# Softmax steps cut into parts between adding steps, and eight columns' sums moved from TensorE to VectorE and the crossbar

## The chip, the cores and the metric

The kernel runs on one core of one Trainium2 chip. The metric is the device time of one execution in microseconds (us); the median of several executions is quoted. The engines are TensorE (PE; its weight loads are listed as PEld), VectorE (DVE), ScalarE (ACT), GpSimd (POOL) and SyncE (SP), besides the DMA engines. The "crossbar" is the DMA path that transposes a tile while it moves it. "PE's use of unit u" means the start of PE's first matmul that reads unit u's transposed tile.

## The reference, cut to what matters

```python
# x: 8 x 4160 x 192, weight_gen: 8 x 4160 x 8 x 7
w = exp(weight_gen - max) ; w = w / (sum over the 7 taps + 1e-9)
y[b, s, h, :] = sum over k of w[b, s, h, k] * x_padded[b, s + k, h, :]     # causal window of 7
h1, h2 = y @ moe_w1, y @ moe_w2                                           # 192 -> 1024
out = maximum(h1, h2) @ moe_w_out                                         # 1024 -> 192
```

## The kernel before

The 33280 rows lie as 128 partitions by 260 columns, in batches of 16 columns (batch 16 has 4). A unit is a piece of a batch: 4 columns in batches 0 and 1 (units 0 to 7), 8 columns later (units 8 to 35), 4 in the last (unit 36). For each batch ScalarE takes exp of the seven taps' logits, DVE sums them (`red`), ScalarE takes Ln of the sums, DVE subtracts it from the logits (`shift`), and ScalarE's second exp (`weights`) gives the normalised weights `en_t` in bf16. For each unit DVE multiplies the seven shifted windows of x by the weights (`mul`) and sums the seven products in three adds (`adds`), and the crossbar turns `y_t` into `yt`:

```python
    def adds(b, o, first=False):
        ...
        nc.vector.tensor_tensor(out=taps(0, 1, 3), in0=taps(0, 1, 3), in1=taps(3, 1, 3), op=ALU.add)
        if first:
            return
        ...
        nc.vector.tensor_tensor(out=taps(0, 2, 2), in0=taps(0, 2, 2), in1=taps(1, 5, 2), op=ALU.add)
        nc.vector.tensor_tensor(out=_sub(y_ts[b], ...), in0=taps(0, 1, 1), in1=taps(2, 1, 1), op=ALU.add)
```

For the first 32 columns the crossbar is not used: DVE does only the first add (`first=True`) or none, and `sum_transpose` on PE sums the four remaining taps (all seven where DVE added none) and transposes them in one go, by matmuls with an identity; ScalarE copies the result to `yt`.

PE then computes h2 - h1 and ScalarE its ReLU, in groups of three tiles (a tile is one column's worth of work), and PE adds y @ (w1 @ w_out) and relu(h2 - h1) @ w_out, which together are the output. ScalarE copies the results out of PSUM and issues the stores. ScalarE carries out its queue in order: ReLUs, result copies, the softmax's exp and Ln all stand in one line.

What runs ahead is written into the loop over tiles by `extra(t)`:

```python
        if s == 0 and b + 1 < NB:
            c = b + 1
            mul(c, 0)
            if c + 1 < NB:
                shift(c + 1)
            adds(c, 0)
        if s == 8 and b + 2 < NB:
            mul(b + 1, 8)
            if b + 3 < NB:
                red(b + 3)
            adds(b + 1, 8)
        ...                                   # weights(c, 0), weights(c, 8) at tiles 8 and 12 of a batch
        if s == 14 and 3 < b + 3 < NB:
            ln(b + 3)
```

The softmax here doesn't subtract the row's maximum and nothing guards it: scores larger than these inputs give would overflow.

## Time and profile before

| | before |
|---|---|
| time, median (range) | 418.81 us (418.5 to 419.28, 4 runs) |
| busy: PE / DVE / ACT | 403.7 / 378.0 / 359.8 us of a span of 417.0 |
| DVE's last `y_t` ends | 385.1 us |
| DVE for 16 columns | 23.84 us |
| slack between landing of `yt` and PE's use, units 8 / 22 / 30 | 10.7 / 6.0 / 0.13 us |

The first line below is from the page's chain of work that ended last, by engine (share of the span). The others are from the table of waits: who waited for what, total us, number of waits, the longest.

```profile
DVE 73%; PE 17%; issue 4%; ACT 3%; DMA 2%; SPq 1%; DVEq 0%
```

```profile
ACT rd_t L260 <- PE hd L250: 30.3, 70, 0.8
...
PE op_ps L302 <- ACT o_t L346: 2.5, 6, 0.5
...
PE hd L250 <- ACT rd_t L260: 0.9, 3, 0.3
```

ScalarE waits for PE, in small pieces; PE hardly waits at all. Yet the chain that led to the last instruction runs through DVE for 73% of the span. Both are true: DVE has no pause for 360 us and PE has next to none, and at unit 30 they meet: `yt` lands 0.13 us before PE's use of it, and PE waits 0.24 us.

### The profile page before, as it was taken

Reading aid. Unit: us, or ns where it says so; the run is one execution under the profiler, and the core shown is the slowest. Engines: PE = TensorE matmul, PEld = TensorE weight load, DVE = VectorE, ACT = ScalarE, POOL = GpSimd, SP = SyncE. Lnnn points to the kernel's source line nnn. Section 1 sums busy time; section 2 is a strip of 40 time slices with the busy share of each in tenths; the row PEclk is TensorE's granted clock in tenths of the full one; section 3 lists DMA queues with packets and bytes.
Section 4 is the critical chain, followed back from the end, with each engine's and each line's share of the span. In section 5 each row is a group of like instructions: output and inputs, shape, how many; then the busy total and the mean of one; then the engine's idle time right before and its main releaser. Section 6 shows DMA issues by size and latency. Waiting matters only on the chain.

```text
span 417.0 us, 15881 instructions
## 1 busy us (share of the span) xinstructions
PE 403.7 (97%) x7369; PEld 326.8 (78%) x7369; DVE 378.0 (91%) x177; ACT 359.8 (86%) x416; POOL 69.0 (17%) x102
## 2 busy tenths in 40 slices
PE   7989999999999999999999999999999999999995
PEld 7878899777777778777787777877778677777795
DVE  5999999999999999999999999999999999999000
ACT  5898989999999899898989899899998898887871
POOL 1510101221201122212112232200113221120000
PEclk9999999999999999999999999999999999999999
DMA  8965427867569756875866669557674787685213
GB/s 235 260 168 169 108 68 169 183 153 129 144 151 181 192 151 163 207 147 153 201 149 147 168 127 242 142 163 198 142 209 64 165 202 151 128 163 115 97 49 144
DMA packets 60242, 65.68 MB, mean 157 GB/s; under 512 B 47601, under 2 KB 48497, under 8 KB 60176
## 3 DMA queue, kind: packets, MB, share of 16 engines
q0 software_dynamic: 8128, 24.11, 28.3%
q1 hardware_dynamic: 46720, 15.30, 21.5%
q10 hardware_dynamic: 5328, 25.27, 15.8%
q8 instruction: 57, 0.93, 0.9%
q14 instruction: 9, 0.07, 0.1%
HBM read 35.96 MB, written 25.56 MB: 148 GB/s over the span
## 4 chain that ended last, share of the span: by engine, by line
DVE 73%; PE 17%; issue 4%; ACT 3%; DMA 2%; SPq 1%; DVEq 0%
DVE m_t L157 36%; DVE m_t L172 15%; DVE m_t L177 11%; PE op_ps L290 8%; PE hd L250 5%; DVE sum_t L132 3%; DVE y_t L179 3%; DVE wg_t L140 3%; DMA ws1T<-in_moe_w_dram 2%; PE op_ps L302 2%; ACT rd_t L260 1%; PE hdp L250 1%; PE yps L218 1%; ACT en_t L148 0%; SPq L480 0%
## 5 line engine op out<-in xcount | busy, mean ns | idle before, releaser
L260 ACT ACTIVATE rd_t<-hd 128x1024 bf16<-128x1024 f32 (+1 forms) x206 | 234.6, 1183 | 30.8 <-PE hd L250 30.3
L290 PE MATMUL op_ps<-wo,rd_t 64*128 64x192 bf16 x4160 | 210.3, 243 | 0.1
L290 PEld LDWEIGHTS <-rd_t 64*128 64x128 bf16 x4160 | 180.1, 94 | 16.2 <-ACTq L323 0.3
L250 PE MATMUL hd<-yt,wd 64*128 64x512 bf16 (+1 forms) x1584 | 187.2, 360 | 1.1 <-ACT rd_t L260 0.9
L157 DVE TENSOR_TENSOR m_t<-xb_t,en_t 128x10752 bf16<-128x10752 bf16 (+1 forms) x37 | 187.5, 5070 | 0.2 <-ACT en_t L148 0.2
L250 PEld LDWEIGHTS <-wd 64*128 64x128 bf16 x1776 | 92.8, 94 | 42.3 <-issue 1.4
L194 POOL CAST gate<-yt 128x1 f32<-128x1 bf16 x29 | 33.2, 1146 | 280.8 <-DMA yt<-y_t 280.8
L172 DVE TENSOR_TENSOR m_t<-m_t 128x4608 bf16<-128x4608 bf16 (+1 forms) x34 | 79.5, 2339 | 0.1
L346 ACT COPY o_t<-op_ps 128x384 f32<-128x384 f32 (+1 forms) x99 | 56.9, 585 | 8.2 <-PE op_ps L290 8.1
L302 PE MATMUL op_ps<-w,yt 64*128 64x192 bf16 x780 | 55.3, 243 | 3.2 <-ACT o_t L346 2.5
L302 PEld LDWEIGHTS <-yt 64*128 64x128 bf16 x780 | 38.6, 94 | 20.1 <-issue 5.6
L177 DVE TENSOR_TENSOR m_t<-m_t 128x3072 bf16<-128x3072 bf16 (+1 forms) x29 | 50.2, 1730 | 1.0
L148 ACT ACTIVATE en_t<-wg_t 128x896 bf16<-128x896 f32 (+1 forms) x37 | 34.1, 935 | 1.9 <-ACT o_t L346 1.2
L179 DVE TENSOR_TENSOR y_t<-m_t 128x1536 bf16<-128x1536 bf16 (+1 forms) x29 | 27.4, 944 | 1.0
L336 DVE COPY o_t<-op_ps 128x192 f32<-128x192 f32 x1 | 0.4, 358 | 27.9 <-ACT o_t L336 27.9
L115 POOL DMA_DIRECT2D xb_t<-in_x_dram x32 | 17.2, 539 | 24.8 <-DVE m_t L157 16.1
L132 DVE TENSOR_REDUCE sum_t<-e_t 128x128 f32<-128x896 f32 (+1 forms) x17 | 17.6, 1037 | 2.9 <-ACT e_t L127 2.9
L127 ACT ACTIVATE e_t<-wg_t 128x896 f32<-128x896 f32 (+1 forms) x17 | 15.8, 928 | 3.3 <-DMA wg_t<-in_weight_gen_dram 2.8
L140 DVE TENSOR_TENSOR wg_t<-wg_t,sum_t 128x896 f32<-128x896 f32 (+1 forms) x17 | 17.7, 1043 | 0.8 <-ACT sum_t L135 0.8
L260 ACT ACTIVATE rd_t<-hdp 128x1024 bf16<-128x1024 f32 x16 | 15.7, 1027 | 1.5 <-PE hdp L250 0.5
L218 PE MATMUL yps<-ident,m_t 128*64 128x128 bf16 x492 | 15.3, 220 | 0.3 <-DVE m_t L157 0.2
L218 PEld LDWEIGHTS <-m_t 128*64 128x64 bf16 x492 | 14.1, 110 | 1.9 <-issue 1.1
(45 smaller groups left out, 85.6 us busy)
## 6 DMA issues: line engine op xcount, KB each, us to landing
out_dram<-o_t ACTq DMA_DIRECT2D x28, 768.0 KB, 4.3
xb_t<-in_x_dram POOLq DMA_DIRECT2D x28, 384.0 KB, 4.9
wg_t<-in_weight_gen_dram POOLq DMA_DIRECT2D x14, 448.0 KB, 6.3
xb_t<-xb_t POOLq DMA_DIRECT2D x16, 288.0 KB, 5.4
out_dram<-o_t ACTq DMA_DIRECT2D x8, 384.0 KB, 3.2
wg_t<-in_weight_gen_dram SPq DMA_DIRECT2D x2, 448.0 KB, 5.3
xs<-in_x_dram SPq DMA_DIRECT2D x2, 384.0 KB, 6.8
xb_t<-in_x_dram POOLq DMA_DIRECT2D x1, 768.0 KB, 6.8
```

The lines of the kernel that those rows point to most:

```text
L148: nc.scalar.activation(out=_sub(en_ts[b], o * WGC * 2, [[2 * N, K], [2, N], [1, 2]]), in_=_sub(wg_ts[b], o * WGC, [[1, K], [K, N], [0, 2]] ...
L157: nc.vector.tensor_tensor(out=m_t[:, K * o * D:K * (o + n) * D], in0=_sub(xb_ts[b], o * D, [[D, K], [1, n * D]]), in1=_sub(en_ts[b], o * W ...
L172: nc.vector.tensor_tensor(out=taps(0, 1, 3), in0=taps(0, 1, 3), in1=taps(3, 1, 3), op=ALU.add)
L177: nc.vector.tensor_tensor(out=taps(0, 2, 2), in0=taps(0, 2, 2), in1=taps(1, 5, 2), op=ALU.add)
L179: nc.vector.tensor_tensor(out=_sub(y_ts[b], o * D, [[64, 2], [P, 3 * w // 2], [1, 64]]), in0=taps(0, 1, 1), in1=taps(2, 1, 1), op=ALU.add,)
L194: nc.gpsimd.tensor_copy(out=gate, in_=yt[:, 0:1])
L218: nc.tensor.matmul(yps[half(j), k * P:(k + 1) * P], lhsT=m_t[:, at:at + 64], rhs=ident, start=(t == taps[0]), stop=(t == taps[-1]), skip_g ...
L250: nc.tensor.matmul(hid_out(t, f, j), lhsT=wd[half(j), s * F + f * P:s * F + (f + 1) * P], rhs=_sub(yt_ts[u][half(j), :], (s + j) % 3 * P, ...
L260: nc.scalar.activation(out=rd[:, k * 1024:(k + n) * 1024], in_=hd[:, at:at + n * 1024], func=AF.Relu)
L290: return nc.tensor.matmul(op_out(c), lhsT=rd[half(r), k * 1024 + at:k * 1024 + at + P], rhs=wo[half(r), f * D:(f + 1) * D], start=False, s ...
L302: nc.tensor.matmul(op_out(c + j), lhsT=yt_ts[u][half(j), (3 * i + (s + j) % 3) * P:(3 * i + (s + j) % 3 + 1) * P], rhs=w10[half(j), s * D: ...
L346: nc.scalar.copy(out=_sub(o, c % 24 * D, [[D, len(qs)], [h * D, 2], [1, D]]), in_=_sub(tile_, at + (qs[0] - p) * D, [[D, len(qs)], [512, 2 ...
```

## The change

The intent: (a) a softmax step set between two adds that depend on one another hides the second one's wait for the first, so the shift is cut into three parts and the reduction into two, one ahead of each add. (b) With the time won, DVE sums columns 24 to 31 (units 6 and 7) wholly and the crossbar moves them, which frees PE of two `sum_transpose` calls and ScalarE of two copies. (c) Ln is issued two tiles later from batch 6 on, because the reduction ends later now.

```diff
+    def part(b, i, of):
+        n = BATCHES[b][1]
+        h0, h1 = n * i // of * H, n * (i + 1) // of * H
+        return slice(h0, h1), h0 * K, [[K, h1 - h0], [1, K]]
 ...                                     # red(b, i, of) and shift(b, i, of) work on such a part
-    def adds(b, o, first=False):
+    def adds(b, o, first=False, beside=lambda i, of: None):
 ...                                     # beside(0, 3), beside(1, 3), beside(2, 3) ahead of the adds
     def rest_of_1():
-        adds(1, 8, True)
+        adds(1, 8)
     def end_of_1():
-        adds(1, 12, True)
+        adds(1, 12)
-        6: (lambda: (weights(2, 8), ln(3), sum_transpose(6, LEFT)), lambda: load_x(3, 0, 8)),
-        7: (lambda: sum_transpose(7, LEFT), none),
+        6: (lambda: (weights(2, 8), ln(3), transpose(6)), lambda: (transpose(7), load_x(3, 0, 8))),
 ...
+        at = 14 if t <= 16 * 3 else 16
+        c = (t - at) // 16 + 3
+        if (t - at) % 16 == 0 and 3 < c < NB:
+            ln(c)
-            if c + 1 < NB:
-                shift(c + 1)
-            adds(c, 0)
+            adds(c, 0, beside=lambda i, of: shift(c + 1, i, of) if c + 1 < NB else None)
-            if b + 3 < NB:
-                red(b + 3)
-            adds(b + 1, 8)
+            adds(b + 1, 8, beside=lambda i, of: red(b + 3, i, 2) if b + 3 < NB and i < 2 else None)
-        if s == 14 and 3 < b + 3 < NB:
-            ln(b + 3)
```

## The prediction

> **What bounds the kernel now.** I read the page's busy shares first, then the table of waits, then the timelines of VectorE (DVE), ScalarE (ACT) and TensorE (PE).
>
> ```profile
> PE 403.7 (97%) x7369; PEld 326.8 (78%) x7369; DVE 378.0 (91%) x177; ACT 359.8 (86%) x416; POOL 69.0 (17%) x102
> ```
>
> Three engines are nearly full, so the question is who waits for whom. The table of waits has almost nothing for PE and DVE, but two small rows tell that they are coupled:
>
> ```profile
> PE hd L250 <- DMA yt<-y_t: 0.2, 1, 0.2
> ...
> ACT sum_t L135 <- DVE sum_t L132: 3.9, 4, 1.4
> ```
>
> DVE makes each unit of eight columns (`y_t`), the crossbar moves it into `yt`, PE uses it. Following each unit through the trace, I took the landing of `yt` and PE's first matmul with it. The slack between them is 10.7 us for unit 8 (lands 65.1, used 75.8), 7.7 us for unit 14, 6.0 us for unit 22, 1.8 us for unit 28, 0.5 us for unit 29 and 0.13 us for unit 30 (lands 329.44, used 329.58); units 31 to 35 have 0.7 to 3.3 us and the last one 10.8 us. PE thus starts with a lead of DVE's results that it uses up, because DVE needs 23.84 us for 16 columns (its multiplications start at 47.66, 71.49, 95.33 us) and PE about 22.9 us at full speed. DVE has no pause above 0.04 us from 25 to 385 us. PE is the bound by a hair, and DVE stands right behind it by unit 30.
>
> One pair of units on DVE, late in the run (start, duration in us):
>
> ```profile
> 339.40 1.08 DVE L140 TENSOR_TENSOR wg_t<-wg_t,sum_t 128x896 f32<-128x896 f32 x1
> 340.40 2.55 DVE L172 TENSOR_TENSOR m_t<-m_t 128x4608 bf16<-128x4608 bf16 x1
> 342.99 1.76 DVE L177 TENSOR_TENSOR m_t<-m_t 128x3072 bf16<-128x3072 bf16 x1
> 344.78 0.96 DVE L179 TENSOR_TENSOR y_t<-m_t 128x1536 bf16<-128x1536 bf16 x1
> 345.65 5.75 DVE L157 TENSOR_TENSOR m_t<-xb_t,en_t 128x10752 bf16<-128x10752 bf16 x1
> 351.32 0.38 DVE L132 TENSOR_REDUCE sum_t<-e_t 128x32 f32<-128x224 f32 x1
> 351.62 2.54 DVE L172 TENSOR_TENSOR m_t<-m_t 128x4608 bf16<-128x4608 bf16 x1
> ```
>
> Start-to-start times count here, not durations. An instruction that needs nothing of the one before it starts 0.08 us before that one ends (the add at 340.40 in front of an end at 340.48); a dependent one starts 0.04 us after the end (342.99 after 342.95). A dependence thus costs 0.12 us.
>
> **What the Trainium skill says.** "Perfetto Trace Analysis", section on the DVE / Act engine instruction: the profiled time runs to the write's acknowledgement, while the next instruction may already begin when the ALUs are done. This trace agrees: that is the 0.08 us overlap, and a dependent successor loses it. "Vector Engine (DVE) Microarchitecture Reference", section 5.2: about 75 ns per instruction after queue overlap, plus 1.04 ns per column. The trace agrees: start to start, 224 elements take 0.30 us and 896 take 1.00 us, so 1.04 ns each and a fixed 0.07 us. "VectorE: DVE Perf Modes", the section on the DRAIN, says a semaphore after each instruction costs nothing extra; the 0.12 us here disagrees, and the measurement decides. "Perfetto Trace Analysis", the section on optimizing Scalar/DVE operations, recommends breaking up instructions where the engine is not saturated; this DVE is.
>
> **The change part by part.**
>
> (1) Parts on DVE. The shift of 896 elements becomes 280, 280 and 336, one ahead of each add: 0.07 x 3 + 0.93 = 1.146 us for 1.00, so +0.146. It breaks two dependences (first to second add, second to third), each worth 0.12: -0.24. Net -0.096. The reduction becomes two halves: +0.073, one dependence broken, -0.12; net -0.05. A batch of 16 columns gains 0.146 us, and some 13 batches give -1.9 us of DVE by the end.
>
> (2) Columns 24 to 31 (units 6 and 7) wholly on DVE. The first add of 2304 elements took 1.27 us start to start (46.39 to 47.66). With dependent followers, as in the last unit, it is 1.39, then 0.99, then 0.48: 2.86 us. Twice +1.59 gives +3.18 us on DVE, between 41 and 51 us, where it delays everything later on DVE. I call DVE's delay D: 3.18 us at batch 3's shift, less 0.146 a batch, so 1.6 at batch 14, 1.4 at batch 15 and 1.3 at the end.
>
> (3) The same on PE and ACT: these sums and transposes vanish,
>
> ```profile
> 46.92 1.53 PE L218 MATMUL yps<-ident,m_t 128*64 128x128 bf16 x48
> ...
> 51.58 1.53 PE L218 MATMUL yps<-ident,m_t 128*64 128x128 bf16 x48
> ```
>
> 1.46 us start to start each, 2.9 us of PE, and two ACT copies of 0.8 us. So from 53 us PE and ACT run 2.9 us earlier than before. With PE at 97% one is tempted to book 2.9 us. But this is a lead over DVE, and the lead is what runs out later.
>
> (4) Results of the softmax come later within a unit. For batches of 16, `en_t` of columns 0 to 7 reads the first two shift parts (560 of 896 elements; its 448 lie within them, and in the built program only the second half waits for DVE anew). The second part ends 0.36 + 2.47 + 0.44 = 3.27 us after the first starts, against 1.08: +2.2 us. The reduction's end moves from 1.08 to 0.54 + 2.47 + 0.62 = 3.62: +2.5 us. Ln is put off by two tiles, from batch 6 on, to allow for this, but in groups of three tiles that moves it by a whole group for some batches and not at all for batches 8, 11 and 14.
>
> ACT runs its queue in order, so a late shift or reduction stalls the ReLUs behind it, and PE after them. Slack before the change, measured in the trace:
>
> ```profile
> 339.68 1.88 ACT L260 ACTIVATE rd_t<-hd 128x2048 bf16<-128x2048 f32 x1
> 341.58 1.04 ACT L148 ACTIVATE en_t<-wg_t 128x896 bf16<-128x896 f32 x1
> 342.52 1.01 ACT L260 ACTIVATE rd_t<-hd 128x1024 bf16<-128x1024 f32 x1
> 343.46 0.80 ACT L346 COPY o_t<-op_ps 128x768 f32<-128x768 f32 x1
> ```
>
> This `en_t` (batch 15) starts 1.10 us after its shift ended at 340.48. After the change the two parts end at 340.48 + 1.43 + 2.2 = 344.1, so it cannot start before: ACT is then 2.5 us later than before, whatever lead it had. Ln of batch 14 (306.54, reduction ended 304.72) comes out alike: 304.72 + 1.62 + 2.54 = 308.9, 2.3 us later. `en_t` of batch 12 (slack 2.97) gives 1.1 us later, the landing of unit 30 gives D = 1.5 less 0.13, so 1.4 us later. These are limits on the same clock; they don't add. The latest wins: 2.5 us.
>
> Sum: ACT can absorb little. The copy at 343.46 ends at 344.26 and PE takes the bank at 344.54, so 0.2 us. After that PE has no idle time to catch up with except 0.3 us at 353.3, where ACT waited for the last batch's reduction; Ln of that batch now comes a group later. The end moves by 2.5 - 0.2 - 0.3 = +2.0 us: 418.8 + 2.0 = 420.8 us.
>
> **The rivals.**
>
> PE decides, and its 2.9 us are gained: 415.9 us. For it: 97% busy, and waits for `yt` of 0.2 us in the whole run. Against it: those 0.2 us at unit 30 show that PE can't run earlier there than DVE lets it; with D positive there is nothing to take.
>
> The broken dependences are worth more than 0.12 us, so that D is gone before unit 28 or so: then 417 to 418.5 us. For it: parts as fine as these have no example in this trace but the 224-element ones. Against: the fixed 0.07 us fits both kinds of instruction.
>
> Only the landing of `yt` counts, since ACT's stall hides in its 14% idle time: +1.4 us, less the 0.3, so about 419.9 us. For it: ACT waits 30 us for PE in 70 small pieces. Against: in the group of 341 us ACT has 0.2 us to give.
>
> The crossbar's landing grows, from two more transposes and a second load of batch 3's first half, which the new transpose of unit 6 issues in addition to the old one: landing varies between 2.7 and 7.4 us already. Those additions lie at 45 to 60 us, where slack is 10 us; no effect, unless phases shift late: up to 423 us.
>
> **Range and chances.** The central path gives 420.8, the DVE-only path 419.9, so I say 420.6. A stall that hides wholly and a larger gain per part would make 418; two stalls that do not overlap with one another, or later landings, 422.6. No path reaches 2% (8.4 us): faster 0.01, same 0.97, slower 0.02.
>
> **What would show it.** DVE's last `y_t` should end near 386.4 (385.07 before); a pair of units should take 23.7 us instead of 23.84. PE should be 2.9 us early for unit 8 and lose this lead by some 260 us; ACT should show new waits for DVE's `wg_t` (batches 12 and 15) and `sum_t` (8, 11, 14) of 1 to 2 us each, and PE waits for ACT behind them. I am wrong if PE keeps its lead to the end, if parts cost clearly other than 0.07 us more each, or if `en_t` waits for nothing.

## The result, and the profile after

The changed kernel took 421.25 us (420.84 to 421.84, 4 runs) against 418.81. The ratio is 1.0058, with a 95% interval of 1.0041 to 1.0076: by the threshold of 2% the same, by the interval slower by about 2.4 us. Ratios here are the mean time of one kernel's fast runs over that of the other's fast runs of the same rounds, so not quite the ratio of the medians.

The page after, busy shares and chain by engine:

```profile
PE 401.5 (96%) x7273; PEld 324.6 (77%) x7273; DVE 380.1 (90%) x222; ACT 358.6 (85%) x414; POOL 70.2 (17%) x106
...
DVE 68%; PE 20%; issue 4%; DMA 4%; ACT 2%; SPq 1%; DVEq 0%
```

PE has 2.2 us less to do, DVE 2.1 us more, and the span is 3.0 us longer (420.06 against 417.03). The work that was saved lay on an engine that did not get to use it.

The table of waits after:

```profile
ACT sum_t L142 <- DVE sum_t L139: 6.4, 6, 1.4
...
PE op_ps L313 <- ACT o_t L357: 4.2, 9, 0.6
...
ACT en_t L155 <- DVE wg_t L147: 1.3, 2, 0.6
...
PE hd L261 <- DMA yt<-y_t: 1.2, 1, 1.2
```

Against before: ScalarE's waits for DVE's sums rose from 3.9 to 6.4 us, waits for DVE's shift are new, PE's waits for ScalarE's copies rose from 2.5 to 4.2 us, and its wait for `yt` from 0.2 to 1.2 us.

DVE in the timeline of the changed kernel, the same unit as in the prediction's excerpt (start, duration in us):

```profile
340.46 0.44 DVE L147 TENSOR_TENSOR wg_t<-wg_t,sum_t 128x280 f32<-128x280 f32 x1
340.82 2.55 DVE L181 TENSOR_TENSOR m_t<-m_t 128x4608 bf16<-128x4608 bf16 x1
343.29 0.44 DVE L147 TENSOR_TENSOR wg_t<-wg_t,sum_t 128x280 f32<-128x280 f32 x1
343.65 1.75 DVE L187 TENSOR_TENSOR m_t<-m_t 128x3072 bf16<-128x3072 bf16 x1
345.32 0.50 DVE L147 TENSOR_TENSOR wg_t<-wg_t,sum_t 128x336 f32<-128x336 f32 x1
345.74 0.95 DVE L190 TENSOR_TENSOR y_t<-m_t 128x1536 bf16<-128x1536 bf16 x1
346.61 5.75 DVE L164 TENSOR_TENSOR m_t<-xb_t,en_t 128x10752 bf16<-128x10752 bf16 x1
```

Read the starts. The first add now takes 2.47 us from start to start (340.82 to 343.29) where it took 2.59, the second 1.67 where it took 1.79, and the parts take 0.36, 0.36 and 0.42 us. From the first part to the next multiplication it is 6.15 us; before, from shift to multiplication, 6.25 us.

ScalarE at the Ln of batch 14, ahead of unit 29, and PE at unit 30, in the timeline of the changed kernel (in brackets the idle time before, and what ended it):

```profile
305.65 1.90 ACT L271 ACTIVATE rd_t<-hd 128x2048 bf16<-128x2048 f32 x1
308.58 0.31 ACT L142 ACTIVATE sum_t<-sum_t 128x128 f32<-128x128 f32 x1 [1.03 <-DVE sum_t L139]
308.80 1.00 ACT L271 ACTIVATE rd_t<-hd 128x1024 bf16<-128x1024 f32 x1
```

```profile
332.06 1.47 PE L261 MATMUL hd<-yt,wd 64*128 64x512 bf16 x12 [1.19 <-DMA yt<-y_t]
```

A Ln of 0.3 us stands in the queue ahead of a ReLU and waits 1.03 us for its reduction; the ReLU behind it is late by as much. The last line is PE's wait for unit 30.

PE's use of a unit, in us, from the two traces:

| unit | 8 | 16 | 17 | 20 | 23 | 26 | 29 | 30 | 33 | 36 |
|---|---|---|---|---|---|---|---|---|---|---|
| before | 75.80 | 166.86 | 178.06 | 213.21 | 247.56 | 282.73 | 317.08 | 329.58 | 364.42 | 398.76 |
| after | 73.60 | 164.69 | 176.63 | 212.54 | 247.62 | 283.53 | 318.62 | 332.06 | 366.41 | 400.76 |
| difference | -2.20 | -2.17 | -1.43 | -0.67 | +0.06 | +0.80 | +1.54 | +2.48 | +1.99 | +2.00 |

PE starts 2.2 us ahead and loses it in steps of 0.7 us. Each step up to unit 29 follows a wait of ScalarE: Ln of batches 8, 11 and 14 (waits of 1.09, 1.10 and 1.03 us at 167, 238 and 309 us), `en_t` of batches 9 and 12 (0.64 us each at 202 and 273 us). At unit 30 PE waits for the crossbar itself. The profiled execution is the slowest of the four (421.84 us); of the 3.0 us in its span, 2.0 lie ahead of the end of the last result copy and 1.0 behind it, where only the last stores are left.

The slack went at once, not slowly. Unit 8's `yt` landed 10.7 us before its use in the kernel before and lands 2.4 us before it now, because DVE is 3.0 us later, PE 2.2 us earlier and the move itself 3.0 us longer (8.3 us). At unit 18 the slack is 0.16 us.

### The profile page after: what moved, and what is told of

It reads as the page before. It is cut to its first block, busy times and chain, and to the rows that moved or that the text cites. A ratio compares the mean times of both kernels' runs of the same rounds, so it can differ in the third digit from the quotient of the medians.

```text
span 420.1 us, 15743 instructions
## 1 busy us (share of the span) xinstructions
PE 401.5 (96%) x7273; PEld 324.6 (77%) x7273; DVE 380.1 (90%) x222; ACT 358.6 (85%) x414; POOL 70.2 (17%) x106
## 4 chain that ended last, share of the span: by engine, by line
DVE 68%; PE 20%; issue 4%; DMA 4%; ACT 2%; SPq 1%; DVEq 0%
DVE m_t L164 34%; DVE m_t L181 14%; DVE m_t L187 10%; PE op_ps L301 10%; PE hd L261 8%; DVE sum_t L139 3%; DVE wg_t L147 3%; DVE y_t L190 3%; DMA yt<-y_t 2%; PE op_ps L313 2%; DMA ws1T<-in_moe_w_dram 2%; ACT rd_t L271 1%; SPq L491 0%; ACT w1t L612 0%; DVE wd L527 0%
## 5 line engine op out<-in xcount | busy, mean ns | idle before, releaser
L187 DVE TENSOR_TENSOR m_t<-m_t 128x3072 bf16<-128x3072 bf16 (+1 forms) x31 | 51.9, 1674 | 0.1
L190 DVE TENSOR_TENSOR y_t<-m_t 128x1536 bf16<-128x1536 bf16 (+1 forms) x31 | 28.4, 916 | 0.6
L147 DVE TENSOR_TENSOR wg_t<-wg_t,sum_t 128x280 f32<-128x280 f32 (+4 forms) x45 | 22.0, 489 | 0.8 <-ACT sum_t L142 0.8
L139 DVE TENSOR_REDUCE sum_t<-e_t 128x64 f32<-128x448 f32 (+2 forms) x30 | 19.6, 652 | 2.9 <-ACT e_t L127 2.9
L261 PE MATMUL hdp<-yt,wd 64*128 64x256 bf16 x192 | 12.7, 270 | 0.0
L229 PE MATMUL yps<-ident,m_t 128*64 128x128 bf16 x396 | 12.2, 220 | 0.5 <-DVE m_t L164 0.4
```

Source lines behind the costliest of these rows:

```text
L147: nc.vector.tensor_tensor(out=w_t, in0=w_t, in1=_sub(s_ts[b], hs.start, [[1, hs.stop - hs.start], [0, K]]), op=ALU.subtract)
L190: nc.vector.tensor_tensor(out=_sub(y_ts[b], o * D, [[64, 2], [P, 3 * w // 2], [1, 64]]), in0=taps(0, 1, 1), in1=taps(2, 1, 1), op=ALU.add,)
L261: nc.tensor.matmul(hid_out(t, f, j), lhsT=wd[half(j), s * F + f * P:s * F + (f + 1) * P], rhs=_sub(yt_ts[u][half(j), :], (s + j) % 3 * P, ...
```

## The experiments

Each call had its own chip and its own runs of the kernel before, so compare by the ratio or with that call's median: 418.55 us for e1 to e4, 419.92 for e5 to e8, 418.77 for e9 and e10, 419.03 for e11 and e12. In each call single runs of the kernel before lay up to 7 us above its quickest (418.2 to 425.7 us over all), which makes the intervals wide. One of them in each of the first two calls (425.03 and 425.68 us) is in that call's median, but in no ratio.

**e1: the columns on VectorE, the softmax steps whole**, with Ln placed as in the kernel before.

```diff
-        at = 14 if t <= 16 * 3 else 16
+        at = 14
-   adds(c, 0, beside=lambda i, of: shift(c + 1, i, of) if c + 1 < NB else None)
+   adds(c, 0, beside=lambda i, of: shift(c + 1) if c + 1 < NB and i == 0 else None)
-   adds(b + 1, 8, beside=lambda i, of: red(b + 3, i, 2) if b + 3 < NB and i < 2 else None)
+   adds(b + 1, 8, beside=lambda i, of: red(b + 3) if b + 3 < NB and i == 0 else None)
```

> Columns 24 to 31 on VectorE and the crossbar, softmax steps whole as before. Theory (VectorE's added 3.2 us set the end through the landing of yt): nothing earns the 3.18 us back, unit 30's yt lands 3.2 us later than in the kernel before and its slack there was 0.13 us, so the end is 3.0 us later, about 421.8 us; TensorE waits for yt for more than 1 us in all near 330 us. Rival A (the parts, with softmax results late for ScalarE, are the loss): without parts the saved TensorE work shows, 416.6 to 418.8 us.

Measured: 422.97 us (422.49 to 427.65), ratio 1.0126 (1.0089 to 1.0164). That is 1.2 us later than expected and far from rival A's range: the columns alone cost more than the whole change, so the parts are not the loss. In e1's trace DVE is 2.87 us late at unit 8 and at the end, and PE's use of unit 36 is 2.87 us late too. The wait that carries it is not the one I named. In e1's table of waits:

```profile
ACT sum_t L142 <- DVE sum_t L139: 8.7, 6, 2.0
...
PE hd L261 <- DMA yt<-y_t: 0.6, 1, 0.6
```

PE's only wait for `yt` is at 107 us; near 330 us there is none, for unit 30 landed 5.0 us after its issue here and not 7.4. ScalarE instead waits 1.98 us each for the reductions of batches 10 and 13. VectorE's lateness reaches PE through whichever of its results is needed first.

**e2: the parts and the later Ln, the columns on TensorE as before.**

```diff
-        adds(1, 8)
+        adds(1, 8, True)
-        adds(1, 12)
+        adds(1, 12, True)
-        6: (lambda: (weights(2, 8), ln(3), transpose(6)), lambda: (transpose(7), load_x(3, 0, 8))),
+        6: (lambda: (weights(2, 8), ln(3), sum_transpose(6, LEFT)), lambda: load_x(3, 0, 8)),
+        7: (lambda: sum_transpose(7, LEFT), none),
```

> Softmax steps in parts and the later Ln, columns 24 to 31 summed and transposed on TensorE as before. Theory: VectorE gains 0.17 us per 16 columns and is 1.9 us ahead by unit 30; the later parts cost ScalarE nothing because that gain pays for them; TensorE is the bound and loses only its waits at unit 30 (0.24 us) and at 353 us (0.31 us), so 418.3 us, 0.5 us below before. Rival A (parts are the loss): 420 to 421 us, with ScalarE waiting about 1 us each for the reductions of batches 8, 11 and 14.

Measured: 418.20 us (418.08 to 419.57), ratio 0.9993 (0.9978 to 1.0008). As expected in size, though the interval holds 1. Its chain of work that ended last:

```profile
PE 74%; ACT 16%; issue 3%; DVE 2%; DMA 2%; SPq 1%; ACTq 1%; DVEq 0%
```

DVE's share of the chain falls from 73% to 2%: with the parts alone DVE's last `y_t` ends at 383.0 us, 2.0 us earlier, and DVE is no longer on the path. But PE stands on it with 402.5 us of work, so those 2.0 us turn into 0.4 us of time by the medians. The share on the chain fell by 71 points for that: it says which engine is last, not by how much.

**e3: all but the last adding step of columns 24 to 31 left out**, a wrong result, to see what TensorE's saving is worth when VectorE doesn't pay for it.

```diff
+        if b == 1 and o >= 8 and not first:
+            ...                              # only y_t = tap 0 + tap 2
+            return
```

> The changed kernel, but for columns 24 to 31 only the last of the three adding steps is done (a wrong result on purpose): VectorE's added 3.18 us become minus 1.5 us, TensorE's saving and the crossbar moves stay. Theory: with VectorE not late the TensorE lead of 2.2 us lasts to the end, and the waits at unit 30 and 353 us are gone too: about 416.2 us, no wait of ScalarE for sums above 0.3 us after 100 us. Rival B (TensorE's saving is worth nothing, or the crossbar moves and the doubled load cost the time): 418.5 to 421 us.

Measured: 418.94 us (418.26 to 419.52), ratio 1.0005 (0.9992 to 1.0018). A miss by 2.7 us, on the side of rival B. The timelines of DVE and of POOL in e3 show what I had overlooked:

```profile
71.31 5.76 DVE L164 TENSOR_TENSOR m_t<-xb_t,en_t 128x10752 bf16<-128x10752 bf16 x1 [1.94 <-DMA xb_t<-xb_t]
```

```profile
53.41 9.83 POOL L213 CAST gate<-yt 128x1 f32<-128x1 bf16 x1 [7.31 <-DMA yt<-y_t]
63.17 0.53 POOL L115 DMA_DIRECT2D xb_t<-in_x_dram  x1
63.70 0.54 POOL L121 DMA_DIRECT2D xb_t<-xb_t  x1
```

VectorE waited 1.94 us for batch 3's x: the doubled load of it was issued only after POOL's one-element cast behind unit 7's move, and that cast took 9.83 us. VectorE's lead was gone at 71 us, so e3 tested something else than meant. PE kept 2.0 us of its own lead up to unit 31 and lost 1.8 us of it at units 32 and 33, where `en_t` of batch 15 waited 1.08 us for its shift and unit 33's move took 9.2 us. e6 repeats it cleanly.

**e4: Ln of batches 8, 11 and 14 a group later.**

```diff
-        at = 14 if t <= 16 * 3 else 16
-        c = (t - at) // 16 + 3
-        if (t - at) % 16 == 0 and 3 < c < NB:
-            ln(c)
+        for at in (14, 16, 18):
+            c = (t - at) // 16 + 3
+            if (t - at) % 16 == 0 and 3 < c < NB and at == (14 if c < 6 else 18 if c % 3 == 2 else 16):
+                ln(c)
```

> The changed kernel with the Ln of batches 8, 11 and 14 one more group of tiles later. Theory (the limits of ScalarE's waits and of yt lie on one clock and don't add, the latest decides): the three waits of 1.0 to 1.1 us go, TensorE keeps its lead longer, and unit 30 takes it all back: 421.0 us, within 0.3 us of the changed kernel. Rival C (the stalls add up): minus 2.2 us, about 419 us.

Measured: 431.65 us and a wrong result. In program order this Ln stands after the shift that should read it, so the shift took the plain sums. Nothing follows from its time. e7 is the mended version.

**e5: the changed kernel without the doubled load.**

```diff
-  lambda: (transpose(7), load_x(3, 0, 8))
+  lambda: transpose(7)
```

> The changed kernel without the second load of batch 3's first half (the crossbar move of unit 6 already starts that load). Theory: the doubled load lies at 61 to 67 us and only delays landings there, where nothing binds; 421.0 to 421.5 us, the same as the changed kernel. Rival (the doubled load is part of the loss): 1 us or more below that.

Measured: 421.89 us (421.16 to 422.25), ratio 1.0039 (0.9994 to 1.0084). Within its wide interval the same as the change, so the doubled load is no large part of the loss. Its profile is of use for another reason: unit 30 landed in time, and `en_t` of batch 15 was the longest of the late waits:

```profile
343.92 1.04 ACT L155 ACTIVATE en_t<-wg_t 128x896 bf16<-128x896 f32 x1 [1.09 <-DVE wg_t L147]
```

The prediction had put the end of this wait at 344.1 us. Behind it PE waited another 0.26 us for unit 33, whose move took 8.3 us. PE's use of unit 36 was at 400.91, against 400.76 in the changed kernel, where unit 30 did it. Different last waits, nearly the same end.

**e6: e3 without the doubled load.**

> As e3 (only the last adding step of columns 24 to 31, wrong on purpose), and without the doubled load, for which VectorE waited 1.94 us at 71 us in e3. Theory: VectorE keeps its 2.1 us lead at unit 8 and has over 4 us at unit 30, so TensorE's lead of 2.2 to 2.7 us lasts to the end: 416.2 us, and no wait of ScalarE for sums or shifts after 100 us. Rival B (TensorE's saving is worth nothing): 418 us or more.

Measured: 416.54 us (416.03 to 417.49), ratio 0.9918 (0.9877 to 0.9959), and a chain with PE in front:

```profile
PE 74%; ACT 17%; issue 4%; DVE 2%; DMA 2%; SPq 1%; ACTq 1%; DVEq 0%
```

As expected, and rival B is out. TensorE's saved work is worth some 2 us, as long as VectorE doesn't fall behind for it; the rest of the gain belongs to the parts (e2: PE's use of unit 36 is at 397.64 there). The wrong result doesn't matter for this reading, since every other instruction is in place. PE's use of unit 36 is at 395.17, 3.6 us earlier than in the kernel before and 2.5 us earlier than in e2.

**e7: e4 mended**, the multiplication, shift and adds of the unit being written two tiles later too; DVE's own order is unchanged.

```diff
  (the edit of e4, and)
-        if s == 0 and b + 1 < NB:
+        if s == 2 and b + 1 < NB:
```

> The changed kernel with the Ln of batches 8, 11 and 14 one group of tiles later, and the shift of the batch written after it this time (VectorE's order is as in the changed kernel). Theory (the limits lie on one clock and the latest decides): ScalarE's waits of 1.0 to 1.1 us for these reductions go; unit 30's yt, or en of batch 15, takes the lead back: 420.8 to 421.3 us. Rival C (stalls add up): each of the three waits took 0.7 us of TensorE, so 2.1 us less, about 419.1 us.

Measured: 422.78 us (421.24 to 424.26), ratio 1.0061 (1.0017 to 1.0105). The median is above my range, on a chip whose runs of before are 1.1 us slower as well; the ratio is that of the change. The three waits for reductions are gone from the profile, and nothing is won, so rival C is out (its 419.1 us would be a ratio of 1.0007 to 418.81, below the interval): `en_t` of batch 15 waits 1.33 us, and PE waits 1.25 us for unit 33. The profiled execution holds an accident. TensorE's clock was granted at half for 3.4 us at 36 us, and PE used unit 8 at 76.88 us, 3.3 us later than in the changed kernel; unit 36 it used at 401.85, only 1.1 us later. An early lead of PE, or its loss, mostly vanishes on the way. But a PE that is 3.3 us late would hide the three waits in any case; that the placing removes them is seen in e12, which has it too, ran without such an accident and shows none of the three.

**e8: e7, and the shift in 448, 224 and 224 elements.**

```diff
  (the edits of e7, and)
+        if of == 3:
+            h0, h1 = ((0, n // 2, 3 * n // 4, n)[j] * H for j in (i, i + 1))
```

> As e7, and the shift in parts of 448, 224 and 224, so that en of the first eight columns needs only the part ahead of the first add. Theory: neither Ln nor en can wait now, the only limit left is the landing of yt, with VectorE 1.1 to 1.3 us late at unit 30: 419.8 to 420.8 us, TensorE's one wait over 1 us is for yt near 330 us. Rival C: 418.5 us or less.

Measured: 420.91 us (419.70 to 427.23), ratio 1.0028 (0.9969 to 1.0087). Unclear: the interval holds both the change and no loss at all. Rival C asks for 418.5 or less, and no run was below 419.7.

**e9: only columns 28 to 31 on VectorE, with e8's placing.**

```diff
  (the edits of e8, and)
-        adds(1, 8)
+        adds(1, 8, True)
-        6: (lambda: (weights(2, 8), ln(3), transpose(6)), ...
+        6: (lambda: (weights(2, 8), ln(3), sum_transpose(6, LEFT)), ...
```

> Only columns 28 to 31 on VectorE, 24 to 27 back on TensorE; the Ln of batches 8, 11 and 14 a group later and the shift in parts of 448, 224, 224 as in e8. Theory: VectorE pays 1.59 us at the start and has earned it back (0.17 us a batch) by unit 29 or so, TensorE saves 1.1 to 1.5 us; the limit at unit 30 is then about 0.4 us before that of the kernel before, and the waits at unit 30 and 353 us go: 417.2 to 418.0 us against 418.6, faster than both kernels by a little. Rival (any work moved to VectorE shows in the end): 419 us or more.

Measured: 419.11 us (418.50 to 424.61), ratio 0.9997 (0.9940 to 1.0055). Not the gain I expected. The median lies just inside the rival's range of 419 us or more, but beside its own runs of before (418.77) it is level, and the interval leaves both open. In its profile, one of the slower executions (421.51 us), the moves of units 28 to 30 landed 8.1, 8.4 and 10.6 us after their issue and PE waited 3.6 us for them.

**e10: parts with e8's placing, the columns on TensorE.**

> Parts with the later Ln and the 448, 224, 224 split as in e9, columns 24 to 31 on TensorE. Theory: VectorE is ahead from the start and TensorE alone decides, as in e2: 418.2 us, within 0.3 us of e2; a better placing of the softmax is worth nothing where ScalarE never waits for it. Rival (the placing itself is worth time): below 417.5 us.

Measured: 418.19 us (418.08 to 418.72), ratio 0.9958 (0.9921 to 0.9994), a correct result. The time is e2's, so the placing itself is worth nothing, as expected. The ratio flatters it: 5 of the 11 runs of before in that call took 420.4 to 422.8 us, and against its median the gain is 0.6 us.

**e11: the changed kernel with its output stores cut to 8 of 128 partitions**, so that crossbar moves and stores don't meet. Its output is wrong, which doesn't matter for the time.

```diff
-  ap=[[CPP * D, P], *ap]),   in_=_sub(o_t[0], c % 24 * D, ap),
+  ap=[[CPP * D, 8], *ap]),   in_=_sub(o_t[0][0:8, :], c % 24 * D, ap),
```

> The changed kernel with every output store but the last unit's cut to 8 of 128 partitions (wrong on purpose; the number of stores and ScalarE's work stay), so that the crossbar moves meet no store. Theory (two limits on one clock): yt lands within 5 us of issue and no longer waits, but Ln of batch 14 and en of batch 15 still hold ScalarE about 2 us behind the kernel before: 420.2 to 420.9 us, ScalarE's waits of about 1 us for sums of batches 8, 11, 14 and about 1 us for the shift of batch 15 stay. Rival D (the collision of stores and crossbar moves is the whole loss): 416.3 to 417.5 us.

Measured: 419.42 us (419.36 to 419.63), ratio 0.9981 (0.9930 to 1.0032). 0.8 us below my range, 1.9 us above rival D's. From its table of waits:

```profile
ACT sum_t L142 <- DVE sum_t L139: 6.8, 6, 1.4
PE op_ps L313 <- ACT o_t L357: 5.7, 12, 0.7
...
ACT en_t L155 <- DVE wg_t L147: 2.9, 4, 1.2
```

The waits for `yt` are gone (no row), ScalarE's waits for DVE are all there and larger, and PE's use of unit 36 is at 399.97, still 1.2 us later than before. With the stores nearly empty the stretch behind it is 0.7 us shorter (a span of 417.5 for a use at 399.97, 417.0 for one at 398.76), which my range had left out. So the softmax's way through ScalarE delays PE by itself, and the crossbar adds at most 0.8 us in the profiled run of the change (400.76 less 399.97); DVE itself is 0.3 us earlier in e11's trace (its last `y_t` ends at 385.53, not 385.85), so part of that may not be the crossbar's.

**e12: e11 with e8's placing.**

> As e11, with e8's placing too (Ln of batches 8, 11, 14 later, shift in 448, 224, 224), VectorE's 3.2 us of added work still there. Theory: with both limits lifted nothing connects VectorE's lateness to TensorE any more, its lead of 2.2 us lasts: 416.2 to 416.9 us, no wait for yt, sums or shifts above 0.3 us after 100 us. Rival E (a further wait takes their place): 418 us or more.

Measured: 417.56 us (417.18 to 417.91), ratio 0.9935 (0.9888 to 0.9981). Faster than e11 by 1.9 us, so the placing does matter once the crossbar can't take its place as the last wait. But it is above my range, and rival E has a point. PE's use of unit 36 is at 398.41, only 0.35 us earlier than before. ScalarE waits 1.50 us for the reduction of batch 15 and 1.24 us for the shift of batch 15: with PE 2.2 us ahead, the next of DVE's results in line became the limit. In its timeline of ScalarE:

```profile
332.23 0.31 ACT L144 ACTIVATE sum_t<-sum_t 128x128 f32<-128x128 f32 x1 [1.50 <-DVE sum_t L141]
341.09 1.04 ACT L157 ACTIVATE en_t<-wg_t 128x896 bf16<-128x896 f32 x1 [1.24 <-DVE wg_t L149]
```

`en_t` of batch 16 waits another 1.23 us at 368 us, and PE once 0.45 us for `yt`, at 245 us. I had called the limits lifted; they were only moved.

## Why the prediction was right

The time, 421.25 us, lies in the range of 418.0 to 422.6, 0.65 us above the 420.6 stated and 0.45 above the 420.8 of the sum. By its steps:

- **Parts on DVE.** Right. Each broken dependence gave 0.12 us, each extra instruction cost 0.07 us. A batch takes 23.67 us instead of 23.84, a gain of 0.17 where 0.146 was booked.
- **The columns on DVE.** Right. Unit 8's last add starts 3.05 us later (61.75 against 58.70), with 3.18 less one pair of parts expected. By the end DVE is 0.8 us late (385.85 against 385.07); the sum had 1.3; the larger gain per batch, some 13 times, explains 0.3 of the difference. The 0.12 us were read rightly, but not what the Trainium skill says beside them (last section).
- **PE's lead.** The term of 2.9 us was mis-sized: it measured 2.2 us. When PE came earlier, it waited 0.91 us for a ReLU at 51.4 us. The lead was gone by unit 23, at 248 us, where the prediction had some 260. Since the lead runs out, its size did not matter for the end.
- **Late softmax results through ScalarE.** Right for Ln of batches 8, 11 and 14 and `en_t` of batch 12; `en_t` of batch 9 waits too, which I hadn't named, and that of batch 15, which I had, waits only where unit 30 lands in time (e5). The waits for the shift are 0.64 us, below the 1 to 2 us forecast. Each wait cost PE about 0.7 us.
- **Which limit comes last.** Here the profiled run differs. I had `en_t` of batch 15 as the latest limit (2.5 us) and unit 30's landing as an earlier one (1.4 us), with the move taking 7.4 us as before. It took 8.8 us, with DVE 1.1 us late there instead of 1.5, and unit 30 came out at +2.5 us, the same lateness. e5 shows the path that I had named. That both ways come to nearly the same lateness is why the number held, and that is luck.
- **The limits don't add.** Shown by e7 (a placing without the three waits of about 1 us, no time won), by e5 (other last waits, nearly the same end), and by e8, e11 and e12 together: e8's placing wins 1.9 us with small stores, and with full ones nothing that its wide interval shows.
- **The rival "PE decides".** Its 415.9 us is what e6 comes near to (416.54), with VectorE's work taken away and the parts' share in it. So the gain existed, and VectorE's 3.2 us were its price. Against the rival "the stall hides in ScalarE's idle time" stands e11: with the crossbar's waits gone PE was still 1.2 us late.
- **The crossbar's landing.** I held the additional moves for harmless at a slack of 10 us, unless phases shift late. The moves grew at once, from 5.3 to 8.3 us at unit 8, and stayed longer: the median of all is 5.8 us, before 4.7. PE waited for one only at unit 30.
- **The 0.45 us above the sum.** In the profiled run PE's use of unit 36 is 2.0 us late, just what the sum says, and another 1.0 us comes behind the last result copy, with the last stores. Why these take longer is not known, and the other three runs have no trace.

Where the expected gain of 2.9 us went can be named. PE got 2.2 us of it, and gave back 4.2 us in steps (it ends 2.0 us late) as VectorE's results, due later by 3.1 us at the start and by some 1.1 us at unit 30, came up in ScalarE's queue and at the crossbar.

A version that beats both kernels: e10 (and e2, of the same median) with 418.2 us, correct. That is 3 us below the change; below the kernel before it is 0.4 to 0.6 us by the medians, which e2's interval doesn't separate from nothing.

## What to carry to other kernels

When two engines are both nearly full, find the slack between producer and consumer at several points of the run: a lead that shrinks steadily tells which engine is slower, and work moved to that engine costs its full length once the lead is gone, however busy the other one looks. Breaking a dependence on a full engine is worth its 0.12 us per place, but a result delivered later within the unit can stall an in-order queue far away, so list the first reader of each result before moving it. Removing one wait out of several limits on the same clock gains nothing until the latest of them is gone.

## What the Trainium skill lacked or had wrong

- "VectorE: DVE Perf Modes", the section on the DRAIN: it reports that eight copies took as long with a semaphore after each as with one after the last. The prediction said that the 0.12 us here disagrees; it does not. In the trace of the kernel before, all but one of DVE's 177 instructions update a semaphore, those too whose successor starts 0.08 us before their end. What costs the 0.12 us is to wait for the instruction directly before, and for that the section has no size: with an independent part between two adds the first took 2.47 us instead of 2.59.
- "DMA: Bandwidth & Descriptors", section DMA Transpose (X-bar), gives no time for a crossbar move beside ordinary stores; the page's rules only say that a transpose next to ordinary DMAs needs nothing. In the kernel before, 12 moves that met no store (none in flight between 1.5 and 2.5 us after the issue) landed after 3.7 us in the median and 16 that met one after 5.6 us; in the changed kernel 27 of 30 met one, with 6.0 us in the median and 9.1 us at most (the last unit's move is left out; the three others took 3.8, 5.2 and 8.3 us, so stores are not all of it). With small stores (e11) the eight moves whose landing the trace gives took 3.8 to 5.4 us. Why they meet more often in the changed kernel is not shown. With small stores six runs lay within 0.3 us, against 418.4 to 424.4 us for the kernel before; that the collisions make this spread is not shown either, since e10's six runs, with full stores, lay within 0.7 us.
- "Perfetto Trace Analysis", the section on optimizing Scalar/DVE operations, says that GpSimd and DVE share a port that one of them can lock, and refers to the page on SBUF, which has the lock held for a whole instruction. Neither says that a wait can run over several: the same one-element POOL cast took 0.18 us at its shortest and 9.83 us at its longest (e3), beside a DVE that did not pause and carried out five whole instructions in that time, and a load waited behind it. That this port is the cause was not tested.
- "Perfetto Trace Analysis", the section on identifying the most-contended engine, goes by occupancy for VectorE. Here that does not tell the two cases apart: DVE is 91% busy before and 91% busy with the parts alone (e2), and its share of the chain that ended last is 73% in the one and 2% in the other.
